# Four places for the attention chunks, their halves loaded from two queues, and the sign of the float64 weights carried by a leaky ScalarE function

## The chip, the cores and the metric

The kernel runs on one core of one Trainium2 chip. A core has five engines, each with its own instruction stream in order: PE (TensorE, matrix products), DVE (VectorE), ACT (ScalarE), POOL (GpSimd) and SP (SyncE, which here only starts transfers). Sixteen DMA engines move data between the chip's memory and the core's on-chip memory. The engines wait for each other through counting semaphores. The metric is the device time of one execution in microseconds; lower is better.

## What is computed

Three parts run one after the other. A retention layer (attention with a decay in place of the softmax), a dense layer pair with a sigmoid GELU, and a soft mixture of experts:

```python
scores = scale * np.matmul(q, k.transpose(0, 1, 3, 2))      # q, k, v: (8, 8, 576, 64) float32
ret = scores * Dmat                                          # gamma_h ** (i - j) for j <= i, else 0
x = np.matmul(ret, v)                                        # -> x: (4608, 512)
h = x @ w_in                                                 # (512, 2048)
g = h * (1.0 / (1.0 + np.exp(-1.702 * h)))
y = g @ w_out                                                # (2048, 512)
logits = y @ phi                                             # (512, 32)
slot_input = softmax(logits, over tokens).T @ y              # (32, 512), 4 slots for each of 8 experts
slot_out[e] = np.maximum(slot_input[e] @ w1[e], 0.0) @ w2[e] # w1 (8, 512, 1024), w2 (8, 1024, 512)
out = softmax(logits, over slots) @ slot_out                 # (4608, 512)
```

`w_in` and `w_out` come as float64: their generator multiplies a float32 array by a float64 scalar. The kernel turns them into float32 itself, from the two 32-bit halves of each number.

## The kernel before

The 4608 tokens are worked on in 12 blocks of 384. A block needs six attention chunks of 64 tokens (72 chunks in all, 9 for each of the 8 batch entries) and sixteen feature steps (fc 0 to 15, 128 hidden features each).

**A chunk.** `load_chunk(g)` brings the chunk's queries, keys and values into one of the places `packs`: the lower 64 partitions with one DMA (line 171), the upper 64 with another (line 172). `scores(g)` makes the products Sp on PE (lines 183, 184), the scaled keys kt on POOL (187) and the decayed scores on DVE (189, 190), written over the queries. `chunk_out(g)` makes Op on PE (197, 198), scales it into xs on DVE (204), rounds it on ACT (205) and makes the remainder on POOL (206). `state(g)` adds to the running state St on PE (223, 224), and DVE writes the scaled state into the next chunk's place (226, 227). `chunk(g)` runs `chunk_out(g)` and `state(g)`, starts the load of chunk g+3 into the place that chunk g has left, and then runs `scores(g+1)`.

**A feature step.** `main_fc` runs twelve products hp on PE (line 328) and the GELU on ACT into gT (330). Three hp tiles are in use in turn. `turn_fc` turns gT with three DVE transposes (351). After eight steps sixteen small DMAs on SP's queue (357, the "nat block" below) put the turned pieces into `nat`, which the slot product Sg (412) reads in the next block.

**The weights.** `load_raw` loads 512 KB of float64 numbers into one of eight places (six in `early_raw`, two in `raw`). `load_w_in` (16 times) scales the upper words on ACT (276), and DVE shifts the lower words (277), joins the two (278), and puts the sign bit back (279). ACT then rounds the result (282), and POOL or DVE makes the remainder (283; the letters `I` and `Id` in the order below choose). `make_wp` (8 times, two `w_out` pieces each) makes a sign with ACT (293), scales with ACT (294), shifts and joins on DVE (295, 296) and multiplies by the sign on POOL or DVE (297, `O` or `Od`). PE transposes the piece (302, tpw), ACT copies it (303), ACT starts a DMA that keeps the piece in memory (305), and PE and DVE make Wp = w_out phi (310, 312), which the logits Lg (364) need.

**The order.** The list `START` gives the order of the program for the first block: T a load of a chunk, C the constants cs, I a piece of w_in, O a pair of pieces of w_out, A a chunk, M a feature step of block 0. A scheduler then orders the instructions of all engines from that. Block 0 needs chunks 0 to 5 before its first product hp. In later blocks the chunks of block n+1 run between the feature steps of block n, after the steps in `CHUNK_AT`. All DMAs count on eight semaphores (DMAHW0 to DMAHW7) given out in turn over both queues. Before a DMA starts, its engine waits until the DMA that had the same semaphore last has landed.

## Time and profile before

| | us |
|---|---|
| median of three executions | 803.67 (803.54 to 805.54) |
| the profiled execution, its own time | 797.39 |
| its span, first to last instruction | 795.6 |
| PE busy in the span | 727.0 (91%) |
| DVE, ACT, POOL busy | 391.0, 245.4, 186.2 |

The profiled execution is 6.3 us shorter than the median of the others. The span has three parts: a start, in which the weights and the first chunks are prepared and block 0 is worked on (the first product hp begins at 55.2 us), eleven blocks that look alike (to some 664 us), and an end with the experts. PE is the busiest engine by far, and it works nearly without a gap from 60 us on.

### The profile page before, as it was taken

The numbers are of one execution on the slowest core, as the hardware profiler recorded it, in microseconds if no ns is written. First come the engines' busy times: TensorE is split into PE (matmuls) and PEld (weight loads), VectorE is DVE, ScalarE is ACT, GpSimd is POOL, SyncE is SP. The second block draws the span as 40 slices with busy tenths as digits, with TensorE's granted clock in tenths as the row PEclk, the third lists the DMA queues.
The fourth block names the chain that finished last, engine by engine and source line by source line (L and its number), as shares of the span: only waits on it lengthen the run. The fifth ranks groups of instructions, "written<-read, shape, count | busy, mean of one in ns | idle before, by whom it ended". The sixth has DMA issues, their size and how long they took to land.

```text
span 795.6 us, 18020 instructions
## 1 busy us (share of the span) xinstructions
PE 727.0 (91%) x7288; PEld 589.8 (74%) x7288; DVE 391.0 (49%) x1152; ACT 245.4 (31%) x479; POOL 186.2 (23%) x255
## 2 busy tenths in 40 slices
PE   3359999999999999999999999998998999997994
PEld 3247788788788878887888788878877798772453
DVE  3999964545445535454454454543543542222223
ACT  2446552323123223231132232411311323431323
POOL 5664661121221121212221212121122110001000
PEclk9999899999999999999999999999999999998997
DMA  9998867575355644744555447435544559898978
GB/s 230 283 297 247 266 168 187 128 157 130 80 122 122 135 106 106 159 114 96 119 125 132 111 105 160 116 85 119 134 97 99 124 126 324 278 379 341 408 307 325
DMA packets 78003, 142.19 MB, mean 179 GB/s; under 512 B 10720, under 2 KB 52960, under 8 KB 77920
## 3 DMA queue, kind: packets, MB, share of 16 engines
q1 hardware_dynamic: 75616, 136.85, 62.8%
q10 hardware_dynamic: 2304, 4.20, 1.5%
q8 instruction: 57, 0.93, 0.5%
q14 instruction: 26, 0.21, 0.1%
HBM read 92.77 MB, written 13.63 MB: 134 GB/s over the span
## 4 chain that ended last, share of the span: by engine, by line
PE 63%; SPq 15%; DMA 9%; DVE 9%; issue 3%; ACT 1%; POOL 0%; DVEq 0%; POOLq 0%; ACTq 0%
PE hp L328 38%; SPq L357 13%; DMA pack<-in_qkv_dram 8%; PE Sg L412 4%; PE Lg L364 4%; PE Op L197 2%; PE Sp L184 2%; PE h_ps L589 2%; PE so_ps L653 2%; PE St L223 1%; DMA early_raw<-in_moe_w_in_dram 1%; PE op L671 1%; DVE early_raw L278 1%; SPq L171 1%; PE St L224 1%
## 5 line engine op out<-in xcount | busy, mean ns | idle before, releaser
L328 PE MATMUL hp<-x,w 128*128 128x384 f32 x2304 | 445.3, 346 | 2.2 <-ACT x L205 2.2
L328 PEld LDWEIGHTS hp<-x,w 128*128 128x128 f32 x2304 | 399.8, 191 | 32.8 <-issue 10.6
L330 ACT ACTIVATE gT<-hp 128x384 f32<-128x384 f32 x192 | 93.9, 490 | 299.0 <-PE hp L328 297.9
L187 POOL TENSOR_TENSOR kt<-pack,cs 64x256 f32<-64x256 f32 x128 | 83.1, 649 | 215.2 <-DMA pack<-in_qkv_dram 138.8
L351 DVE STREAM_TRANSPOSE ring<-gT 128x128 f32<-128x128 f32 x240 | 55.9, 284 | 127.1 <-ACT gT L330 127.1
L351 DVE STREAM_TRANSPOSE pre<-gT 128x128 f32<-128x128 f32 x288 | 65.4, 281 | 81.3 <-ACT gT L330 77.9
L206 POOL TENSOR_TENSOR x<-xs,x 128x256 fp32r<-128x256 f32 x72 | 56.4, 783 | 195.9 <-ACT x L205 195.1
L197 PEld LDWEIGHTS Op<-pack 128*64 128x64 f32 x576 | 42.2, 144 | 37.4 <-issue 23.8
L205 ACT CAST x<-xs 128x256 fp32r<-128x256 f32 x72 | 29.1, 405 | 126.3 <-DVE xs L204 126.1
L183 PE MATMUL Sp<-pack 128*64 128x64 f32 x576 | 51.9, 233 | 16.9 <-DMA pack<-in_qkv_dram 11.4
L197 PE MATMUL Op<-pack 128*64 128x64 f32 x576 | 53.3, 236 | 12.0 <-DVE pack L189 12.0
L183 PEld LDWEIGHTS Sp<-pack 128*64 128x64 f32 x576 | 43.2, 146 | 18.9 <-issue 11.5
L223 PE MATMUL St<-pack,kt 128*64 128x64 f32 x512 | 47.2, 234 | 9.4 <-DVE pack L227 7.8
L184 PE MATMUL Sp<-pack 128*64 128x64 f32 x576 | 50.3, 233 | 5.6 <-DMA pack<-in_qkv_dram 5.6
L198 PE MATMUL Op<-pack 128*64 128x64 f32 x576 | 51.4, 236 | 0.0
L223 PEld LDWEIGHTS St<-pack,kt 128*64 128x64 f32 x512 | 38.7, 146 | 14.5 <-POOL kt L187 8.9
L364 PE MATMUL Lg<-gT,Wp 128*32 128x384 f32 x384 | 46.5, 502 | 2.5 <-DVE Wp L312 2.5
L184 PEld LDWEIGHTS Sp<-pack 128*64 128x64 f32 x576 | 42.3, 146 | 8.0 <-DMA pack<-in_qkv_dram 7.7
L224 PE MATMUL St<-pack,kt 128*64 128x64 f32 x512 | 44.8, 234 | 0.0
L198 PEld LDWEIGHTS Op<-pack 128*64 128x64 f32 x576 | 41.6, 145 | 0.7 <-DVE pack L190 0.5
L189 DVE TENSOR_TENSOR pack<-Sp,cs 64x256 f32<-64x256 f32 x72 | 30.6, 424 | 19.7 <-PE Sp L184 13.9
L224 PEld LDWEIGHTS St<-pack,kt 128*64 128x64 f32 x512 | 37.6, 147 | 2.6 <-issue 2.6
(125 smaller groups left out, 644.4 us busy)
## 6 DMA issues: line engine op xcount, KB each, us to landing
pack<-in_qkv_dram SPq DMA_DIRECT2D x144, 256.0 KB, 4.7
wx<-in_moe_w_dram SPq DMA_DIRECT2D x56, 512.0 KB, 8.6
nat<-pre SPq DMA_DIRECT2D x192, 96.0 KB, 2.2
nat<-ring SPq DMA_DIRECT2D x160, 96.0 KB, 2.2
out_dram<-ob SPq DMA_DIRECT2D x18, 512.0 KB, 3.4
early_raw<-in_moe_w_in_dram SPq DMA_DIRECT2D x13, 512.0 KB, 9.9
early_raw<-in_moe_w_out_dram SPq DMA_DIRECT2D x11, 512.0 KB, 7.4
wo_dram<-ring ACTq DMA_DIRECT2D x16, 256.0 KB, 6.2
```

The lines of the kernel that those rows point to most:

```text
L183: pe.matmul(Sp[C:128, p, :], t[:, KTA, p], t[:, Q0, p], start=True, stop=True)
L184: pe.matmul(Sp[0:C, p, :], t[:, KTB, p], t[:, Q1, p], start=True, stop=True)
L187: pool.tensor_tensor(kts[g % 2][r0:r0 + C, h], t[r0:r0 + C, KN], ksc[r0:r0 + C, cb, :].unsqueeze(2).to_broadcast([C, NP, D]), op=ALU.mult)
L197: pe.matmul(Op[0:C, p, :], t[:, V0, p], t[:, Q0, p], start=True, stop=True)
L198: pe.matmul(Op[C:128, p, :], t[:, V1, p], t[:, Q1, p], start=True, stop=True)
L223: pe.matmul(s_[0:C, p, :], kk[:, 0, p], t[:, V0, p], start=first, stop=True, skip_group_check=True)
L224: pe.matmul(s_[C:128, p, :], kk[:, 1, p], t[:, V1, p], start=first, stop=True, skip_group_check=True)
L328: pe.matmul(hp, wt[fc][:, a, dc, :], b[n][:, dc, :], start=(i == 0), stop=(i == 3 * NDC - 1))
L330: act.activation(gT[n, g][:, fl, :], hp, AF.Gelu_apprx_sigmoid)
L351: dve.transpose(dst[:, c], src[:, c])
L357: sp.dma_start(nat[n][32 * b:32 * b + 32, :, a, hf * HF:(hf + 1) * HF, :], pre[n, hf][32 * a:32 * a + 32, b])
L364: pe.matmul(Lg[n][32 * fl:32 * fl + 32, :], Wp[:, g * GF + fl, :], gT[n, g][:, fl, :], start=(g == 0), stop=(g == NFC // GF - 1))
```

## The change

- There are four places for chunks (`NPACK` 4), and the load of chunk g+3 stands at the beginning of `chunk(g)`, into the place of chunk g-1.
- The upper half of each chunk is loaded by ACT's queue, the lower half by SP's as before.
- The first two places are set to zero by DVE, the other two by POOL.
- The float64 weights are scaled by ACT's Prelu in place of Copy. It multiplies negative numbers by a further 2^32, which puts a bit into the exponent that the join's shift by three moves to the sign bit. So the DVE step that put the sign back (279), the ACT sign (293) and the product with it (297) are gone, and for `w_out` the scaling is written over the raw piece instead of into the ring.
- There are seven raw places instead of eight, and at the end of the program one place more in `pw2` and one less in `raw`. `Od` in START is now `O`.

```diff
-NW2 = 8
+NW2 = 9
-NPACK = 3
+NPACK = 4
...
-        pool.memset(t[0:C, 0:KN], 0.0)
-        pool.memset(t[C:128, KTA:7], 0.0)
+        own = dve if i < 2 else pool
+        own.memset(t[0:C, 0:KN], 0.0)
+        own.memset(t[C:128, KTA:7], 0.0)
...
         sp.dma_start(t[0:C, KN * PC:7 * PC], qkv[g, 0:C])
-        sp.dma_start(t[C:128, 0:KTA * PC], qkv[g, C:128])
+        act.dma_start(t[C:128, 0:KTA * PC], qkv[g, C:128])
...
     def chunk(g):
 
+        if g + NPACK - 1 < NT // C:
+            load_chunk(g + NPACK - 1)
         chunk_out(g)
         state(g)
-        if g + NPACK < NT // C:
-            load_chunk(g + NPACK)
         if g + 1 < NT // C:
             scores(g + 1)
...
-        if i % 8 < 6:
-            raw = early_raw[:, i % 8]
+        if i % 7 < 6:
+            raw = early_raw[:, i % 7]
         else:
-            raw = px.tile([128, 1024], F32, tag="raw", name="raw", bufs=2)
+            raw = px.tile([128, 1024], F32, tag="raw", name="raw", bufs=1)
...
-            act.activation(w, w, AF.Copy, scale=2.0 ** -112)
+            act.activation(w, w, AF.Prelu, scale=2.0 ** -112, alpha=2.0 ** 32)
             dve.tensor_scalar(lower, lower, 29, None, op0=ALU.logical_shift_right)
-            dve.scalar_tensor_tensor(lower, upper, 3, lower, op0=ALU.logical_shift_left, op1=ALU.bitwise_or)
-            dve.scalar_tensor_tensor(upper, upper, -2147483648, lower, op0=ALU.bitwise_and, op1=ALU.bitwise_or)
+            dve.scalar_tensor_tensor(upper, upper, 3, lower, op0=ALU.logical_shift_left, op1=ALU.bitwise_or)
...
-                bits, sign = wo.bitcast(I32), free
-                act.activation(sign, upper.bitcast(F32), AF.Sign)
-                act.activation(wo, upper.bitcast(F32), AF.Copy, scale=2.0 ** -112)
+                act.activation(upper.bitcast(F32), upper.bitcast(F32), AF.Prelu, scale=2.0 ** -112, alpha=2.0 ** 32)
                 dve.tensor_scalar(lower, lower, 29, None, op0=ALU.logical_shift_right)
-                dve.scalar_tensor_tensor(bits, bits, 3, lower, op0=ALU.logical_shift_left, op1=ALU.bitwise_or)
-                (pool if how["mul"][i] else dve).tensor_tensor(wo, wo, sign, op=ALU.mult)
+                dve.scalar_tensor_tensor(wo.bitcast(I32), upper, 3, lower, op0=ALU.logical_shift_left,
+                                         op1=ALU.bitwise_or)
...
-                    for i in range(2):
-                        prefetch(place_in(px, "raw", 2))
+                    prefetch(place_in(px, "raw", 1))
```

The scheduler's order moves with it. On DVE, in the start, these rows stand around the decayed scores of chunk 3. In the kernel before chunk 3 is in `pack_93` (its scores are lines 189 and 190), and what stands ahead of them, behind the output of chunk 2 (line 204), is this:

```order
L204 TENSOR_TENSOR xs<-Op,cs 128x256
L278 SCALAR_TENSOR_TENSOR early_raw<-early_raw 128x512
L295 TENSOR_SCALAR raw<-raw 128x512
L296 SCALAR_TENSOR_TENSOR ring<-ring,early_raw 128x512
L277 TENSOR_SCALAR raw<-raw 128x512
L279 SCALAR_TENSOR_TENSOR early_raw<-early_raw 128x512
L296 SCALAR_TENSOR_TENSOR ring<-ring,raw 128x512
L278 SCALAR_TENSOR_TENSOR raw<-raw 128x512
L189 TENSOR_TENSOR pack_93<-Sp,cs 64x256
L190 TENSOR_TENSOR pack_93<-Sp,cs 64x256
```

In the changed kernel, whose line numbers differ by one or two, chunk 3 is in `pack_102`, and the same stretch reads:

```order
L205 TENSOR_TENSOR xs<-Op,cs 128x256
L280 SCALAR_TENSOR_TENSOR early_raw<-early_raw 128x512
L190 TENSOR_TENSOR pack_102<-Sp,cs 64x256
L191 TENSOR_TENSOR pack_102<-Sp,cs 64x256
L294 TENSOR_SCALAR early_raw<-early_raw 128x512
```

Seven weight steps stood between the two chunks' rows, and one does now. From the first decayed scores to the xs of chunk 5 there are 68 DVE instructions before and 57 now (lines of the kernel before: 189 and 190 six and seven times, 226 and 227 six and six, 204 six and six, 277 nine and seven, 278 eight and seven, 279 seven and none, 283 four and four, 295 six and four, 296 four and three). On PE the first hp stands behind Op of chunks 0 to 5 in both; the St of chunk 5 and the Sp of chunk 6 now stand ahead of it.

On SP, in the blocks that look alike, around the nat block of block 2's first half (`x16`). Before, with the load of chunk 24 in `pack_93` behind it:

```order
L171 DMA pack_99<-in_qkv_dram 64x1024
L172 DMA pack_99<-in_qkv_dram 64x1024
L357 DMA nat<-pre 32x3x256 x16
L171 DMA pack_93<-in_qkv_dram 64x1024
L172 DMA pack_93<-in_qkv_dram 64x1024
L171 DMA pack_96<-in_qkv_dram 64x1024
```

And now, where chunk 24 is in `pack_93` too:

```order
L172 DMA pack_99<-in_qkv_dram 64x1024
L172 DMA pack_102<-in_qkv_dram 64x1024
L172 DMA pack_93<-in_qkv_dram 64x1024
L356 DMA nat<-pre 32x3x256 x16
L172 DMA pack_96<-in_qkv_dram 64x1024
```

The load of chunk 24 has moved ahead of the sixteen DMAs, and chunk 25 (`pack_96`) is now the first behind them. It is the same at all such places from the fourth nat block on.

On ACT the loads of the upper halves now stand between the GELUs. Here is the stretch with the load of chunk 26 (`pack_99`), with the semaphores that each row waits for:

```order
L329 ACTIVATE gT<-hp 128x384 [waits PE_49] x2
L206 CAST x<-xs 128x4x64 [waits DVE_49]
L173 DMA pack_99<-in_qkv_dram 64x1024 [waits DMAHW5_49,DMAHW6_49,PE_49,Pool_49]
L329 ACTIVATE gT<-hp 128x384 [waits PE_49]
L329 ACTIVATE gT<-hp 128x384 [waits PE_49,Activation_49]
```

The count of DMAHW6 that this load waits for is that of the sixth DMA of the nat block shown above, which SP starts. It stands behind the GELU of step 10 of that block, and the nat block can begin after the GELU of step 7. The loads of the upper halves of other chunks wait in the same way for the sixth, twelfth or last DMA of a nat block, and the first, sixth and eleventh DMA of a nat block wait for an upper half to land.

## Rows read from the trace of the kernel before

**Rows 1.** The page: its first line, and the engines' busy time with their share of the span and number of instructions.
```profile
span 795.6 us, 18020 instructions
...
PE 727.0 (91%) x7288; PEld 589.8 (74%) x7288; DVE 391.0 (49%) x1152; ACT 245.4 (31%) x479; POOL 186.2 (23%) x255
```

**Rows 2.** Five stretches of the span: from and to, length, busy time and instructions of PE, PEld, DVE, ACT and POOL, the granted share of TensorE's clock, the DMA engines' share and GB/s.
```profile
0.00:8.60 8.60, 1.57 (x16) 1.22 (x16) 0.68 (x1) 1.28 (x1) 5.81 (x14) 1.00 0.73 166
8.60:55.20 46.60, 19.93 (x275) 17.20 (x275) 41.80 (x69) 17.52 (x30) 26.47 (x25) 1.00 1.06 285
55.20:128.00 72.80, 69.87 (x823) 59.04 (x824) 61.30 (x136) 42.12 (x78) 42.78 (x41) 0.95 0.80 238
128.00:664.00 536.00, 524.16 (x5288) 440.75 (x5287) 252.16 (x863) 141.62 (x280) 108.27 (x172) 0.99 0.53 122
...
80.00:90.00 10.00, 9.09 (x76) 6.96 (x78) 9.91 (x19) 4.42 (x9) 6.51 (x7) 0.66 0.77 267
```

**Rows 3.** PE's waits from 0 to 128 us: for whom, us in total, how often, the longest.
```profile
PE Op L197 <- DVE pack L189: 12.0, 5, 4.1
PE St L223 <- DVE pack L227: 7.8, 4, 4.4
...
PE Lg L364 <- DVE Wp L312: 2.5, 1, 2.5
```

**Rows 4.** PE's waits from 128 to 664 us, all that there are.
```profile
PE Sp L183 <- DMA pack<-in_qkv_dram: 7.4, 9, 1.5
PE Sp L184 <- DMA pack<-in_qkv_dram: 4.4, 6, 0.8
```

**Rows 5.** DVE's groups of instructions between 8.6 and 55.2 us: count, then busy us and mean ns of one, then idle time before them.
```profile
L279 DVE SCALAR_TENSOR_TENSOR early_raw<-early_raw 128x512 int32<-128x512 int32 x7 | 6.2, 892 | 0.0
L277 DVE TENSOR_SCALAR early_raw<-early_raw 128x512 int32<-128x512 int32 x8 | 4.9, 617 | 2.3 <-DMA early_raw<-in_moe_w_in_dram 2.3
L278 DVE SCALAR_TENSOR_TENSOR early_raw<-early_raw 128x512 int32<-128x512 int32 x7 | 4.8, 688 | 0.4 <-ACT early_raw L276 0.3
L295 DVE TENSOR_SCALAR early_raw<-early_raw 128x512 int32<-128x512 int32 x4 | 4.6, 1155 | 0.1
L283 DVE TENSOR_TENSOR w<-early_raw,w 128x512 fp32r<-128x512 f32 x4 | 3.1, 782 | 0.0
L227 DVE TENSOR_TENSOR pack<-St,cs 64x256 f32<-64x256 f32 x6 | 2.6, 427 | 0.1
L189 DVE TENSOR_TENSOR pack<-Sp,cs 64x256 f32<-64x256 f32 x6 | 2.6, 426 | 4.9 <-DMA cs<-in_consts_dram 4.8
L204 DVE TENSOR_TENSOR xs<-Op,cs 128x256 f32<-128x256 f32 x6 | 2.5, 422 | 1.6 <-PE Op L198 1.5
L190 DVE TENSOR_TENSOR pack<-Sp,cs 64x256 f32<-64x256 f32 x6 | 2.5, 417 | 0.2
L296 DVE SCALAR_TENSOR_TENSOR ring<-ring,early_raw 128x512 int32<-128x512 int32 x3 | 2.5, 818 | 0.0
L226 DVE TENSOR_TENSOR pack<-St,cs 64x256 f32<-64x256 f32 x6 | 2.4, 407 | 0.0
```

**Rows 6.** PE in order of time around 28 us: start us, length us, what; in brackets the idle time before it.
```profile
28.63 0.45 PE L183 MATMUL Sp<-pack 128*64 128x64 f32 x2 [4.00 <-DMA pack<-in_qkv_dram]
```

**Rows 7.** DVE in order of time around 35 us, in the same columns.
```profile
33.40 1.75 DVE L279 SCALAR_TENSOR_TENSOR early_raw<-early_raw 128x512 int32<-128x512 int32 x1
...
36.80 0.43 DVE L189 TENSOR_TENSOR pack<-Sp,cs 64x256 f32<-64x256 f32 x1
```

**Rows 8.** PE in order of time, around the first products hp and at 80 us.
```profile
55.19 0.69 PE L328 MATMUL hp<-x,w 128*128 128x384 f32 x1 [2.15 <-ACT x L205]
...
58.56 2.79 PE L328 MATMUL hp<-x,w 128*128 128x384 f32 x11
...
80.91 1.49 PE L364 MATMUL Lg<-gT,Wp 128*32 128x384 f32 x4 [2.46 <-DVE Wp L312]
82.33 4.21 PE L328 MATMUL hp<-x,w 128*128 128x384 f32 x12
```

**Rows 9.** The chain that ended last, in order of time: start us, length us, what.
```profile
227.21 4.36 PE hp L328 x24
...
547.46 5.93 PE hp L328 x24
...
602.87 5.85 PE hp L328 x24
```

**Rows 10.** SP's queue in order of time around one nat block: start us, length us of the issue, what.
```profile
210.31 11.22 SPq L357 DMA_DIRECT2D nat<-pre  x16
221.64 0.54 SPq L171 DMA_DIRECT2D pack<-in_qkv_dram  x1
222.28 0.55 SPq L172 DMA_DIRECT2D pack<-in_qkv_dram  x1
```

**Rows 11.** PE in order of time behind that nat block.
```profile
225.47 0.30 PE L183 MATMUL Sp<-pack 128*64 128x64 f32 x2 [0.67 <-DMA pack<-in_qkv_dram]
```

**Rows 12.** The page's DMA issues: count, KB each, median us from issue to landing.
```profile
pack<-in_qkv_dram SPq DMA_DIRECT2D x144, 256.0 KB, 4.7
...
nat<-pre SPq DMA_DIRECT2D x192, 96.0 KB, 2.2
```

**Rows 13.** ACT in order of time during that nat block.
```profile
217.05 0.49 ACT L330 ACTIVATE gT<-hp 128x384 f32<-128x384 f32 x1 [1.59 <-PE hp L328]
```

More of the change, by code (lines that the diff above doesn't have):

```diff
@@ L38 @@
 HF = NFC // 2
-NW2 = 8
+NW2 = 9
 NW3, NW4 = 6, 5
 DH = DM // 2
-NPACK = 3
+NPACK = 4
 PC = NP * C
 START = (
-    "T0 C T1 Id T2 P A A Id A I A A I A Id A M O I M A Id M O I M I A M Od I M I A M O Id M I A M O I M Id A M O I "
+    "T0 C T1 Id T2 P A A Id A I A A I A Id A M O I M A Id M O I M I A M O I M I A M O Id M I A M O I M Id A M O I "
     "M A M O M M O M"
@@ L171, in load_chunk @@
         sp.dma_start(t[0:C, KN * PC:7 * PC], qkv[g, 0:C])
-        sp.dma_start(t[C:128, 0:KTA * PC], qkv[g, C:128])
-    how = {"sub": {}, "mul": {}}
+        act.dma_start(t[C:128, 0:KTA * PC], qkv[g, C:128])
+    how = {"sub": {}}
     St = {}
@@ L471, in step @@
         elif x[0] == "O":
-            how["mul"][8 - len(outs)] = x != "Od"
             outs.pop(0)()
```

## The prediction

> **What bounds the kernel now.** I began with the page's first lines: PE is busy for 727.0 of 795.6 us [rows 1], so the change can only win where PE stands still or runs slowly. The table by stretches says where that is [rows 2]. Between 8.6 and 55.2 us PE has 19.9 us of work in 46.6, from 55.2 to 128 it has 69.9 in 72.8, and from 128 to 664 it has 524.2 in 536. In the end, behind 664 us, the change only swaps one place for another, so I leave that part alone.
>
> Next I asked what PE waits for in each stretch. In the start it is DVE: 12.0 us for the decayed scores, 7.8 us for the scaled state [rows 3]. DVE is busy for 41.8 of those 46.6 us [rows 2]: it is the bound. One example shows how. The scores of chunk 3 are made from 28.63 us [rows 6], but DVE gets to them at 36.80, behind weight steps such as a 1.75 us sign step [rows 7]. The DMA engines are also full there, with a share of 1.06 [rows 2], which I return to. From 128 us on, all of PE's waits are for chunks that have not landed, 7.4 + 4.4 = 11.8 us [rows 4], which accounts for the whole of the 11.8 us that PE lacks. SP's rows show the reason: the nat block holds SP's queue from 210.31 for 11.22 us, chunk 24's halves start at 221.64 and 222.28 [rows 10], and PE wants them before they land [rows 11].
>
> **The start, up to the first hp.** The first hp begins at 55.19 us, on the output of chunk 5 [rows 8]. DVE's way to that output is 68 instructions before and 57 now. I price both lists by the means of this stretch [rows 5]. Before: 9 x 0.617 + 8 x 0.688 + 7 x 0.892 + 6 x 1.155 + 4 x 0.818 + 4 x 0.782 + 6 x 2.099 (one each of 189, 190, 204, 226, 227) = 43.2 us. Now: 7 x 0.617 + 7 x 0.688 + 4 x 0.782 + 4 x 1.155 + 3 x 0.818 + 7 x 0.843 + 6 x 1.256 = 32.8 us. The difference is 10.4 us, of which the sign steps are 6.2 and the rest is weight work that now stands behind chunk 5. The lower bound is about 3 us, if DVE then waits for transfers (first rival). The upper bound is 17 us: if the two shift lines, which are the same operation, both took the time of the cheaper one, 4 x 0.538 = 2.2 us more would go, and the 4.8 us in which DVE is now idle might go too. I take 10.4, because DVE, which gives this number, is the engine that is full.
>
> The constants are issued one SP issue earlier, but four upper halves compete with them on the second queue from the first moment. Four halves are 1.0 MB, at 285 GB/s 3.7 us [rows 2, 12]. DVE waits 4.8 us for these constants [rows 5], so a later landing is paid in full: between -0.6 and 3.7, I take 1 us of loss.
>
> DVE's four new memsets cover 64x768. The nearest row writes 64x256 in 0.426 us [rows 5], so each takes at most 1.3 us and all four at most 5.1. DVE has 0.68 us of work up to 8.6 us [rows 2], and that idle time hides them. Prelu I price like the Copy it replaces, one ACT instruction of the same shape; ACT is busy for 17.5 of 46.6 us [rows 2], so a dearer one would be hidden as well.
>
> **The start, from the first hp on.** Here PE is nearly full, so what it has to do moves forward as a whole. One Sp and one St group of a chunk are already done by then; I count 1 us for them. One stall remains that DVE's load causes: 2.46 us for Wp, after which twelve hp take 4.21 us [rows 8] where they take half of 4.36 elsewhere [rows 9]. In those 10 us the granted clock is 0.66 [rows 2]. So 2.5 + 2.0 = 4.5 us hang on Wp coming late. DVE has 11 sign steps and products fewer in this stretch, but its order is new there as well, so I take half, 2 us. The bounds are 4.5 and a new stall of the same size, -4.5.
>
> **The eleven blocks.** Chunk 24 is now started ahead of the nat block, and so are the other chunks that PE waited for. The first chunk behind the block is now one that PE needs a chunk later, that is up to four feature steps of some 2.2 us (half of 4.36) [rows 9], against the 0.7 us that were missing [rows 11]. The upper halves no longer queue on SP at all. I take the whole 11.8 us; the bounds are 6, if only the upper halves come in time, and 11.8. At 547 us twenty-four hp take 5.93 us in place of 4.36 [rows 9], behind such a wait. At 602.87 us it is 5.85 [rows 9]. Together that is 3 us. Few of the fifteen waits [rows 4] were followed by this, so I take half, 1.5, with bounds 0 and 3.
>
> ACT now starts 72 transfers, each shorter than 0.6 us to issue like SP's [rows 10]. It is busy for 31% of the span [rows 1], so the cover is its own idle time in front of each GELU, 1.59 us in the row shown [rows 13]. If the cover were gone, PE would pay up to 72 x 0.6 = 43 us. The wait that comes with them is the third rival. What stands behind a waiting load on ACT is the next GELU, for which PE's three hp tiles wait.
>
> **The sum.** 10.4 - 1 + 1 + 2 + 11.8 + 1.5 = 25.7 us. Against the profiled execution's own 797.4 us this gives 771.7; against the median of 803.67, which lies 6.3 above it, 778.0. I give the second.
>
> **A rule on the second queue.** At the start the DMA engines' share is 1.06 at 285 GB/s [rows 2]. The Trainium skill, DMA: Bandwidth & Descriptors, section Issuing engines are not separate DMA queues, says that transfers from any engine run on the same 16 DMA engines, and that a second issuing engine saves only the time to issue. By that rule the second queue brings the start nothing. The trace of before cannot decide it, since only SP loads chunks there; my sum gives the second queue nothing in the start either, but the first rival is what the rule would mean if the engines were the bound.
>
> **A rule on DVE and POOL.** The shift of line 295 takes 1.155 us in the mean and that of line 277 takes 0.617, for the same shape [rows 5], while POOL is busy for 26.5 us of the stretch [rows 2]. The Trainium skill, SBUF — State Buffer, section SBUF: two separate sides, says that DVE and POOL lock each other out of a shared pair of ports for a whole instruction. By that rule the sign products that leave POOL shorten DVE's other steps as well, and the sum would be up to 2 us larger.
>
> **The rivals.**
> 1. The transfers bound the start. For: the share of 1.06. Against: up to the first hp the new order needs seven chunks, seven pieces of w_in and two of w_out, 3.7 + 3.7 + 1.0 MB and 0.5 of constants, 8.9 MB; at 285 GB/s that is 31 us, against 45 in my forecast. If they decide nevertheless, 3 us remain of the 10.4 and nothing of the 2: 803.7 - (3 + 11.8 + 1.5) + 1 - 1 = 787.4 us.
> 2. Everything goes well: the first hp comes 17 us earlier, the stall on Wp goes whole, and both slow stretches go. 17 + 1 + 4.5 + 11.8 + 3 - 1 = 36.3, so 767.4 us. Against it: every term stands at its end.
> 3. Slower: ACT is caught behind the nat block. The load of chunk 26 waits on ACT for the block's sixth copy. By before's rows that copy is issued near 210.3 + 5 x 0.70 = 213.8 and lands 2.2 us later [rows 10, 12], at 216.0, and ACT would reach it at 217.5 [rows 13]: 1.5 us to spare. PE is covered by two further hp tiles, 2 x 2.2 us. So PE loses only from the point where the copies come 1.5 + 4.4 = 5.9 us later against the GELUs. At 7.5 us each of some 19 nat blocks would cost 1.6 us, 30 us in all: 778 + 30 = 808 us.
> 4. The chunks are late in another way: the waits of rows 4 stay, since the lower halves still queue on SP. Then the start alone is gained: 803.7 - 12.4 = 791.3 us. Against it is the order: the chunk that was late now stands ahead of the block.
>
> **How the numbers follow.** My forecast has a chance of 0.65 with its own range of 772 to 785; rival 1 has 0.14, rival 2 has 0.10, rival 3 has 0.05, rival 4 has 0.06. The range from 766 to 792 takes in the forecast, rivals 1, 2 and 4, and leaves out rival 3 and the ends of the others. A change of under 0.3%, 2.4 us, is about what a measurement of this kernel cannot tell from none. Rival 3 alone is slower; from its 0.05 I give 0.01 to the middle, and 0.01 more for gains that cancel from the other cases: faster 0.94, the same 0.02, slower 0.04.
>
> **What would show it.** The first hp near 45 us and the 193rd (block 1's first) some 13 us earlier than before; no PE wait for a chunk behind 128 us; ACT's waits on loads below a us; lines 279 and 297 gone and DVE below nine tenths by 90 us. The prediction is wrong if the first hp stays beyond 50 us with PE waiting for DMA, if PE waits for ACT's GELU in the blocks, or if DVE's order in the start makes a new stall of several us.

## The result, and the profile of the changed kernel

The changed kernel takes 769.9 us (median of four runs, 768.96 to 770.63) against 803.6 for the kernel before beside it: a ratio of 0.9575, with a 95% interval of 0.9556 to 0.9594. The forecast was 778.0 in a range of 766 to 792. The profiled execution takes 770.2 us of its own; before's took 797.4, so 27.2 us went between the two profiles, where the sum had 25.7. The other 6.6 us of the miss come from the medians: before's three runs lay 6.3 us above its profiled execution, the changed kernel's lie 0.3 below. In four later sets of 7 to 13 runs the kernel before had medians of 798.4 to 802.1, with single runs from 790.4 to 806.8. So the profiled execution of before was an ordinary run, and the 6.3 us that the forecast added lie within the scatter of that kernel.

The page's lines that answer to [rows 1]:

```profile
span 768.4 us, 18070 instructions
...
PE 714.9 (93%) x7288; PEld 581.8 (76%) x7288; DVE 379.2 (49%) x1138; ACT 234.8 (31%) x463; POOL 159.9 (21%) x239
```

The table by stretches, cut where block 1 and the tail now begin, with ten more microseconds around the first products hp and the columns of [rows 2]:

```profile
8.60:55.20 46.60, 22.34 (x318) 20.20 (x319) 32.23 (x65) 15.72 (x28) 21.06 (x27) 0.66 1.06 277
50.00:60.00 10.00, 8.50 (x66) 8.08 (x66) 7.12 (x12) 5.08 (x9) 5.02 (x5) 0.64 1.06 290
55.20:120.00 64.80, 62.81 (x783) 53.17 (x783) 46.02 (x102) 34.18 (x65) 25.20 (x26) 0.98 0.92 272
120.00:635.00 515.00, 515.00 (x5279) 434.95 (x5278) 262.19 (x881) 140.25 (x279) 106.48 (x171) 1.00 0.56 125
```

In the blocks PE stands still no more: 515.00 busy in 515.00, and the view of waits has no row at all for 120 to 640 us, where [rows 4] had 11.8 us. DVE in the start fell from 41.8 to 32.2 us [rows 2]. One thing stands in the first row that the prediction has no term for: the granted clock is 0.66 where before has 1.00 [rows 2]. It falls between 20 and 30 us, where PE is busy for 3.6 of the ten, is 0.50 from 30 to 50 us (the lower of its two levels, 1.2 in place of 2.4 GHz), and is back at 1.00 from 60 us on. No run here separates what that costs. PE's waits up to 120 us, to be laid beside [rows 3]:

```profile
PE hp L327 <- ACT x L206: 10.4, 1, 10.4
PE Op L198 <- DVE pack L190: 9.3, 5, 3.2
PE Sp L184 <- DMA pack<-in_qkv_dram: 7.6, 2, 7.1
PE St L224 <- DVE pack L228: 3.9, 2, 3.1
PE Lg L363 <- DVE Wp L311: 1.1, 2, 0.9
```

The first row is new: one wait of 10.4 us, for the cast of x in front of the first hp. Read from PE in order of time, the two kernels part like this (us):

| | before | changed | difference |
|---|---|---|---|
| first hp | 55.2 | 51.5 | -3.7 |
| first hp to the 193rd (block 1) | 72.75 | 68.6 | -4.2 |
| last GELU of block 0 to that of block 10 | 534.6 | 515.2 | -19.3 |
| the rest | 133.1 | 133.1 | 0.0 |

The stretch from block 1 to 664 us of the kernel before, counted ahead as eleven blocks, holds ten, block 1 to block 10; block 11 lies in the rest. The prediction's term for the eleven blocks is therefore measured on these ten.

**Where the new wait comes from.** ACT in order of time in the changed kernel, from 34 us on:

```profile
34.50 0.68 ACT L278 ACTIVATE early_raw<-early_raw 128x512 f32<-128x512 f32 x1
39.68 0.33 ACTq L304 DMA_DIRECT2D wo_dram<-ring  x1
44.31 0.47 ACTq L173 DMA_DIRECT2D pack<-in_qkv_dram  x1
44.83 0.41 ACT L206 CAST x<-xs 128x256 fp32r<-128x256 f32 x1 [9.65 <-DMA early_raw<-in_moe_w_in_dram]
45.14 0.64 ACT L283 CAST w<-early_raw 128x512 fp32r<-128x512 f32 x1
45.69 0.65 ACT L278 ACTIVATE early_raw<-early_raw 128x512 f32<-128x512 f32 x1
```

DVE in the same time:

```profile
38.98 0.43 DVE L228 TENSOR_TENSOR pack<-St,cs 64x256 f32<-64x256 f32 x1
46.37 1.54 DVE L280 SCALAR_TENSOR_TENSOR early_raw<-early_raw 128x512 int32<-128x512 int32 x1 [6.96 <-ACT early_raw L278]
...
50.60 0.41 DVE L205 TENSOR_TENSOR xs<-Op,cs 128x256 f32<-128x256 f32 x1
```

ACT computes nothing between 35.2 and 44.8 us. At 39.68 it issues a store; next in its queue is the upper half of chunk 8, which starts at 44.31. Each was held (the word used below for an issue that its engine cannot start yet, so that everything behind it in the engine's order waits too). The store waited for a semaphore whose last transfer was a piece of w_out that SP issued at 28.63 and that landed at 39.60. The load carries a wait for a DMA completion semaphore, and the last transfer that used the same semaphore is a piece of w_in that SP issued at 33.43. SP's row of it (it merges two issues), and then the DMA issues of the stretch from 33.4 to 33.7 us, whose last number is the time to landing:

```profile
33.43 1.62 SPq L266 DMA_DIRECT2D early_raw<-in_moe_w_in_dram  x2
```

```profile
early_raw<-in_moe_w_in_dram SPq DMA_DIRECT2D x1, 512.0 KB, 10.8
```

33.43 + 10.8 = 44.23, and 0.08 later ACT goes on. Everything queued behind the load waited with it: a cast of x, a cast of w, the Prelu of the next piece, which had landed at 36.29. DVE was done at 39.4 and then waited 6.96 us for that Prelu. The load held ACT from 40.0 to 44.3, so by an estimate from these rows 4.3 of the 6.96 us are its doing, and 2.7 that of the store in front of it; the output of chunk 5 (line 205) came at 50.60 and the first hp at 51.50.

### The profile page after: what moved, and what is told of

Read it like the earlier page. It is cut to its first block, busy times and chain, and to the rows that moved or that the text cites. A ratio compares the mean times of both kernels' runs of the same rounds, so it can differ in the third digit from the quotient of the medians.

```text
span 768.4 us, 18070 instructions
## 1 busy us (share of the span) xinstructions
PE 714.9 (93%) x7288; PEld 581.8 (76%) x7288; DVE 379.2 (49%) x1138; ACT 234.8 (31%) x463; POOL 159.9 (21%) x239
## 3 DMA queue, kind: packets, MB, share of 16 engines
q10 hardware_dynamic: 8064, 23.07, 12.1%
## 4 chain that ended last, share of the span: by engine, by line
PE 85%; DVE 2%; ACT 1%; issue 1%; DVEq 0%; ACTq 0%
PE hp L327 53%; PE Lg L363 5%; PE Sg L411 5%; PE Op L198 4%; PE Sp L185 3%; PE St L224 3%; PE h_ps L586 2%; PE so_ps L650 2%; PE op L668 1%; PE St L225 1%; PE lt L373 1%; PE tpg L339 1%; PE Op L199 1%; PE Sp L184 1%; PE cp L622 1%; PE dp L398 1%
## 5 line engine op out<-in xcount | busy, mean ns | idle before, releaser
L327 PE MATMUL hp<-x,w 128*128 128x384 f32 x2304 | 438.8, 344 | 11.2 <-ACT x L206 10.4
L327 PEld LDWEIGHTS hp<-x,w 128*128 128x128 f32 x2304 | 396.5, 189 | 40.0 <-ACT gT L329 13.1
L207 POOL TENSOR_TENSOR x<-xs,x 128x256 fp32r<-128x256 f32 x72 | 54.1, 752 | 154.0 <-ACT x L206 153.7
L184 PE MATMUL Sp<-pack 128*64 128x64 f32 x576 | 48.0, 229 | 7.6 <-DMA pack<-in_qkv_dram 7.6
L185 PE MATMUL Sp<-pack 128*64 128x64 f32 x576 | 48.5, 230 | 0.0
L184 PEld LDWEIGHTS Sp<-pack 128*64 128x64 f32 x576 | 41.5, 144 | 7.7 <-issue 7.1
L225 PE MATMUL St<-pack,kt 128*64 128x64 f32 x512 | 44.8, 233 | 0.0
L185 PEld LDWEIGHTS Sp<-pack 128*64 128x64 f32 x576 | 41.5, 143 | 0.3 <-issue 0.3
L411 PE MATMUL Sg<-nat,dn 128*32 128x512 f32 x288 | 37.4, 626 | 0.3 <-DVE dn L400 0.3
```

The source lines that it names most:

```text
L184: pe.matmul(Sp[C:128, p, :], t[:, KTA, p], t[:, Q0, p], start=True, stop=True)
L185: pe.matmul(Sp[0:C, p, :], t[:, KTB, p], t[:, Q1, p], start=True, stop=True)
L225: pe.matmul(s_[C:128, p, :], kk[:, 1, p], t[:, V1, p], start=first, stop=True, skip_group_check=True)
L327: pe.matmul(hp, wt[fc][:, a, dc, :], b[n][:, dc, :], start=(i == 0), stop=(i == 3 * NDC - 1))
L411: pe.matmul(Sg[32 * b:32 * b + 32], dn[n][:, c, :], nv[:, 4 * b:4 * b + 4], start=(c == 0), stop=(c == NT128 - 1))
```

## The experiments

Three parts are told apart: new or old sign steps, three or four places, one or two queues. "Four places" takes in what goes with them: the earlier load, the new zeroing and the seven raw places. The experiments are short edits of the changed kernel or of the one before. Of the eight combinations seven were run; old sign steps with three places and two queues were not. What they gave, with "hp" for the first hp, "block 1" for the 193rd, and "ten" for ten blocks as in the table above:

| kernel | sign | places | queues | median us | hp | block 1 | ten |
|---|---|---|---|---|---|---|---|
| before | old | 3 | 1 | 803.6 | 55.2 | 127.9 | 534.6 |
| e3 | new | 3 | 1 | 793.0 | 52.1 | 121.5 | 537.2 |
| e10 | new | 3 | 2 | 777.1 | 54.4 | 120.9 | 518.9 |
| e11 | old | 4 | 1 | 776.0 | 50.2 | 128.3 | 513.0 |
| e4 | old | 4 | 2 | 782.6 | 55.2 | 134.7 | 516.8 |
| e2, e8 | new | 4 | 1 | 764.3, 762.2 | 45.0, 42.5 | 117.6, 115.5 | 513.4 |
| changed, e7 | new | 4 | 2 | 769.9, 769.8 | 51.5 | 120.1 | 515.2 |

**e1, the start's upper halves on SP.**

```
-        act.dma_start(t[C:128, 0:KTA * PC], qkv[g, C:128])
+        (act if g < 4 or g >= 15 else sp).dma_start(t[C:128, 0:KTA * PC], qkv[g, C:128])
```

> The changed kernel with one difference: the upper halves of chunks 4 to 14 (those loaded in the start) go back to SP's queue; ACT keeps the first four and those of the blocks. Theory A, the held queue: in the changed kernel ACT stood still from 39.68 to 44.31 us in front of chunk 8's upper half, whose completion semaphore was last used by a piece of w_in that SP issued at 33.43 and that takes 10.6 us to land; casts, GELU inputs and the output of chunk 5 stood behind it. Without it the first hp comes 4.6 to 7 us earlier, at 44 to 47 us, and the kernel takes 763 to 766 us. Rival, full DMA engines: their share is 0.99 between 25 and 50 us, so chunks and weights come no sooner whoever issues them; the first hp stays at 50 to 53 us and the kernel at 769 to 772 us. The ten blocks stay at 515 us by both.

Measured: 769.2 us (768.87 to 774.19), the first hp at 50.36. By the numbers the rival won, but ACT's rows show that the hold had only moved, to a store of a piece of w_out:

```profile
41.82 1.42 ACT L293 ACTIVATE early_raw<-early_raw 128x512 f32<-128x512 f32 x2
48.93 0.33 ACTq L304 DMA_DIRECT2D wo_dram<-ring  x1
49.36 0.65 ACT L278 ACTIVATE early_raw<-early_raw 128x512 f32<-128x512 f32 x1 [6.12 <-DMA pack<-in_qkv_dram]
```

The store's semaphore was last used by a lower half that SP issued at 37.07 and that took 11.8 us to land: 48.87. The output of chunk 5 was ready on DVE at 46.43, and ACT cast it at 49.92, behind the store:

```profile
46.02 0.41 DVE L205 TENSOR_TENSOR xs<-Op,cs 128x256 f32<-128x256 f32 x1
```

```profile
49.92 0.39 ACT L206 CAST x<-xs 128x256 fp32r<-128x256 f32 x1
```

So a hold delayed the first hp here too, but since it stayed, the total of e1 could not decide between hold and full engines.

**e2, one queue.**

```
-        act.dma_start(t[C:128, 0:KTA * PC], qkv[g, C:128])
+        sp.dma_start(t[C:128, 0:KTA * PC], qkv[g, C:128])
```

> The changed kernel with both halves of every chunk on SP; the four places and the chunk's load ahead of the nat block stay. Theory A, the order: the eleven blocks were won by starting a chunk ahead of the nat block, not by the second queue. PE still waits for no chunk behind 120 us, the ten blocks take 515 to 517 us, and with ACT free in the start the kernel takes 763 to 767 us. Rival, the second queue: the upper halves queue on SP again and are late again; half of the loss comes back, 6 to 10 us, the ten blocks take 521 to 525 us and the kernel 770 to 778 us.

Measured: 764.3 us (760.86 to 768.05); the first hp at 44.98, ten blocks in 513.4, no wait for a chunk behind 120 us. Theory A holds: no chunk was late, the total lies in its range, and the ten blocks came even shorter than its 515 to 517. With the fourth place the second queue is not needed in the blocks, and in the start it costs.

**e3, the sign alone**, from the kernel before (and the same for w_out, lines 292 to 297):

```
-            act.activation(w, w, AF.Copy, scale=2.0 ** -112)
+            act.activation(w, w, AF.Prelu, scale=2.0 ** -112, alpha=2.0 ** 32)
...
-            dve.scalar_tensor_tensor(lower, upper, 3, lower, ...)
-            dve.scalar_tensor_tensor(upper, upper, -2147483648, lower, ...)
+            dve.scalar_tensor_tensor(upper, upper, 3, lower, ...)
```

> The kernel before with one difference: the leaky function in place of the sign steps (lines 278, 279 and 292 to 297); three places, both halves on SP, eight places for raw weights. Theory A: DVE's list up to the first hp was the bound of the start, so the first hp comes 6.2 us (the sign steps of w_in alone) to 10.4 us earlier, at 45 to 49 us; the waits for chunks in the blocks stay at 11.8 us shown; the kernel takes 803.6 - 12 = 791 us, between 788 and 796. Rival, full DMA engines: DVE gets free but waits for pieces of w_in and chunks; the first hp at 52 us or later, the kernel at 798 to 803 us.

Measured: 793.0 us (789.77 to 802.29 in ten runs), ratio 0.9932 (0.9888 to 0.9977); the first hp at 52.13. The total lies in A's range, the first hp does not: it came 3.1 us earlier in place of 6 to 10. PE's longest waits up to 128 us:

```profile
PE Sp L183 <- DMA pack<-in_qkv_dram: 10.6, 3, 8.8
PE St L223 <- POOL kt L187: 5.8, 1, 5.8
PE Sp L183 <- POOL pack L160: 5.5, 1, 5.5
```

With 0.8 us at line 184 that is 11.4 us for chunks, where before has 5.1. The wait of 8.8 us is for chunk 3, at which before lost 4.0 [rows 6]; but the chunk was no later than before (28.25 us against 28.63), PE only came to it sooner. ACT was held, by stores of line 302:

```profile
36.82 0.65 ACT L281 CAST w<-raw 128x512 fp32r<-128x512 f32 x1 [9.29 <-DMA early_raw<-in_moe_w_out_dram]
48.25 0.40 ACT L205 CAST x<-xs 128x256 fp32r<-128x256 f32 x1 [6.54 <-DMA raw<-in_moe_w_out_dram]
```

DVE's own waits, from its first decayed scores to the output of chunk 5, say where the missing us went:

```profile
DVE early_raw L278 <- ACT early_raw L276: 8.6, 3, 6.1
```

Before, that wait was 0.3 us [rows 5]. DVE was busy for 30.8 us in this stretch in place of 41.3, 10.5 less, and idle for 13.1 in place of 4.8. So waiting for the held ACT took back 8.3 us of the 10.5; for a late chunk DVE did not wait at all.

**e4, the old sign steps**: the diff of e3 the other way round, in the changed kernel, with `Od` back in START.

> The changed kernel with the sign steps of the kernel before; four places, two queues and the early load stay. Theory A: the blocks' gain stays whole (19.4 us for ten blocks), the start gains 0 to 3 us, since DVE is full there again: 781 to 785 us, first hp at 53 to 56 us. Rival, the start's gain came from the second queue and the fourth place and not from DVE: first hp near 51.5 us and the kernel at 770 to 775 us.

Measured: 782.6 us (781.89 to 784.11), the first hp at 55.24, ten blocks in 516.8. Theory A, with 17.8 of the blocks' 19.4 us. Beside the changed kernel's 769.9 the new sign steps are worth 12.7 us with four places.

**e5, no transfer on ACT**, from e2:

```
-                act.dma_start(wo_dram[fc // 2, :, fc % 2, :], wo)
+                pool.dma_start(wo_dram[fc // 2, :, fc % 2, :], wo)
```

> The kernel of e2 (all loads on SP) with one more difference: the stores of w_out's pieces (line 304) are issued by POOL and no longer by ACT, so that ACT issues no transfer at all in the start. Theory A, as e1 and e2 left it: it is any transfer on ACT's queue that holds ACT, a store as well as an upper half, since it waits until the earlier transfer with the same completion semaphore has landed. In e1 ACT stood from 43.24 to 48.93 us in front of a store, in e2 three times before a store, 3.63 + 2.35 + 2.69 = 8.7 us, with DVE waiting for ACT behind it only some 1.6 us of these up to the first hp. So ACT's waits in front of line 304 go, the wait of 3.8 us for the ring copy (line 302) behind the first hp goes, the first hp comes at 42 to 45 us, block 1 some 3 to 6 us earlier than in e2, and the kernel takes 758 to 762 us. Rival, full DMA engines (share 1.07 up to 55 us): ACT waits for pieces of w_in in place of semaphores, block 1 comes within 1 us of e2's 117.6, and the kernel takes 763 to 766 us.

Measured: 764.1 us (763.58 to 766.58), the first hp at 42.82, block 1 at 114.98. The first hp came as theory A said, block 1 hardly (2.6 us before e2, 0.5 before e8), and the total is e2's, 1.9 us above e8's beside it. The holds of stores that were left in e2, the longest from 48.2 to 54.5 us, do not set the time.

**e6, the upper halves on POOL**: the line of e2 with `pool` in place of `sp`.

> The changed kernel with the upper halves issued by POOL in place of ACT; two queues stay. Theory A, the held engine: the second queue costs nothing by itself, what it costs is ACT standing still; with POOL as its engine the hold falls on POOL, behind which only products of kt and remainders of x stand: first hp at 44 to 48 us and 762 to 767 us. Rival, the competition: upper halves that start early on a second queue take the DMA engines from pieces of w_in and from the constants, whoever issues them: first hp at 50 to 53 us, 768 to 772 us. If POOL is slow at issuing (its issue is not in any trace so far) both could be later.

Measured: 767.3 us (764.9 to 770.68), the first hp at 49.48, which fits neither. It answers another question than it asked: POOL starts the first load behind its memsets, and PE gets the upper half of chunk 0 late.

```profile
5.17 2.22 POOL L173 DMA_DIRECT2D pack<-in_qkv_dram  x4
```

PE's view has an 8.31 us wait for it, until 14.30. Inconclusive on the hold.

**e7 and e8, the changed kernel and e2 side by side.**

> The changed kernel itself once more, beside the others of this call on the same chip: 769 to 771 us by every theory, first hp at 51.5 us with ACT standing in front of chunk 8's upper half for 4 to 5 us.

> The kernel of e2 once more beside the changed kernel: theory A says that one queue for the chunks is 4 to 7 us faster than two in the same call (763 to 766 against 769 to 771 us); the rival, that e2's 764.3 was the chip it ran on, says that both are within 2 us here.

Measured: 769.8 us (768.01 to 771.05) and 762.2 (760.31 to 763.83), in one set with e5. The ranges are 4 us apart. One queue with four places is 7.7 us faster than the changed kernel; its ratio to before is 0.9523 (0.9477 to 0.9569), the changed kernel's here 0.9625 (0.9584 to 0.9665).

**e9, the first four upper halves on ACT, no hold.** e5 with `act if g < 4 else sp`.

> The kernel of e5 (ACT issues no transfer later on, the stores go out on POOL) with the upper halves of the first four chunks on ACT, as in the changed kernel; each of these four is the first transfer with its completion semaphore and so waits for none. It has the competition of four early upper halves without the hold. Theory A, the hold: first hp at 42 to 45 us as in e5 (42.8), the kernel at 762 to 766 us. Rival, the competition: the four halves that start at 0.7 us push back the constants and the first pieces of w_in, and all behind them: first hp at 48 to 51 us, near e1's 50.4, the kernel at 766 to 770 us.

Measured: 767.8 us (766.25 to 768.57), the first hp at 46.13, block 1 at 120.96. Both matter. Without a transfer that holds ACT the first hp comes 5.4 us before the changed kernel's; against e5 the four early halves cost 3.3 us there and 6.0 at block 1. DVE's first decayed scores show how it begins, first here, then in e5:

```profile
10.76 0.43 DVE L190 TENSOR_TENSOR pack<-Sp,cs 64x256 f32<-64x256 f32 x1 [5.46 <-DMA cs<-in_consts_dram]
```

```profile
8.04 0.43 DVE L190 TENSOR_TENSOR pack<-Sp,cs 64x256 f32<-64x256 f32 x1 [3.39 <-DMA cs<-in_consts_dram]
```

The constants land 2.7 us later when four halves start beside them. Later on, four waits for GELU cost PE 6.3 us here (1.8 in e5): ACT stands in front of a Prelu whose piece has not landed, and a GELU is queued behind it.

**e10, the second queue without the fourth place**: e3 with `act` for `sp` at the upper half (line 172).

> The kernel of e3 (three places, the leaky function) with the upper halves on ACT: the second queue without the fourth place. Theory A, the place and the order: a load can start only when the chunk's place is free, behind the nat block as before; PE's waits for chunks from 128 us on stay between 6 and 13 us (12.9 in e3) and ten blocks take 525 us or more; ACT is held in the start as in the changed kernel; 785 to 795 us. Rival, the queue: upper halves no longer stand behind the nat block on SP, the waits fall below 4 us, ten blocks take 515 to 520 us and the kernel 770 to 778 us.

Measured: 777.1 us (776.08 to 781.10), ten blocks in 518.9. The rival won. PE's waits from 128 us on, first in e10, then in e3, which has one queue:

```profile
PE Sp L183 <- DMA pack<-in_qkv_dram: 1.4, 3, 0.6
```

```profile
PE Sp L184 <- DMA pack<-in_qkv_dram: 6.5, 6, 2.1
PE Sp L183 <- DMA pack<-in_qkv_dram: 6.4, 9, 1.1
```

The lower halves came no earlier behind the nat block. That of chunk 24 was issued right behind the block and landed 4.1 us later (3.7 in e3), and PE still waited for it:

```profile
216.64 1.13 PE L325 MATMUL hp<-x,w 128*128 128x384 f32 x5
...
218.04 0.24 PE L183 MATMUL Sp<-pack 128*64 128x64 f32 x1 [0.27 <-DMA pack<-in_qkv_dram]
```

But the second wait, for the upper half, is gone, and the new order puts five products hp in front of the chunk's Sp that stood behind it before. So there are two remedies for the late chunks, and either takes nearly all of the waits: a place more, or the upper halves on another queue. The change has both, and pays for the second one in the start. Ten blocks are still 5.5 us longer here than with a fourth place and one queue.

**e11, the old sign steps with four places and one queue.**

> The kernel of e2 and e8 (four places, early load, all loads on SP) with the sign steps of the kernel before: what four places are worth alone. Theory A: DVE bounds the start with the old sign steps whoever issues the loads, so that the sign is worth as much here as beside e4 (782.6 against 769.8, 12.8 us): 773 to 777 us, first hp at 53 to 56 us, no wait for a chunk behind 128 us. Rival: the sign is worth only what e3 showed alone (some 5 us of 798): 766 to 769 us, first hp below 50 us.

Measured: 776.0 us (775.68 to 776.58), ten blocks in 513.0, block 1 at 128.3. Total and blocks are theory A's; the first hp at 50.17 fits neither well. The new sign steps are worth 12 to 14 us here, some of it behind the first hp. Four places alone take some 25 us off (801.5 for before beside it).

**e12, small stores**, from e2:

```
-                act.dma_start(wo_dram[fc // 2, :, fc % 2, :], wo)
+                act.dma_start(wo_dram[fc // 2, :, fc % 2, 0:32], wo[:, 0:32])
...
-            src = wo_dram[key[1]] if wide else ...
+            src = w1[0, 0:128, :].rearrange("p (c d) -> p c d", c=2) if wide else ...
```

> The kernel of e2 and e8 (four places, all loads on SP) with fewer bytes in the start: each of the 16 stores of w_out's pieces writes 32 of its 512 columns, 16 in place of 256 KB, and the pieces read back in the end come from w1 in place of the stored ones (that part of the computation is left out; the number of transfers, their issues and the order of the instructions' kinds stay). Some 13 of the stores are issued before 95 us, 13 x 240 KB = 3.1 MB, at e8's 300 GB/s some 10 us of the engines' time. Theory B, which e1 to e11 suggest, that without the sign steps the transfers bound the start from the first chunk to block 1 (share 1.04 to 1.07 up to 100 us in e8, and block 1 between 115 and 123 us wherever the first hp lies between 42 and 54): block 1 comes 5 to 10 us earlier than e8's 115.5, at 105 to 111 us, and the kernel takes 752 to 758 us. Rival, the engines' order (DVE, ACT and the semaphores) bounds it: block 1 within 2 us of 115.5 and the kernel at 760 to 764 us.

Measured: 766.6 us (766.12 to 769.53), block 1 at 118.3. Theory B falls as it was put: block 1 came 0.7 us later than in e2 and 2.8 later than in e8, not 5 to 10 earlier. But the engines' share hardly moved. Three stretches of e12, then of e8:

```profile
40.00:60.00 20.00, 14.05 (x114) 12.53 (x115) 11.22 (x23) 8.49 (x14) 6.20 (x8) 0.66 1.05 248
60.00:80.00 20.00, 19.05 (x236) 15.76 (x234) 19.38 (x42) 12.27 (x24) 10.35 (x9) 1.00 1.03 270
80.00:100.00 20.00, 17.17 (x230) 14.44 (x232) 18.39 (x42) 12.70 (x26) 8.44 (x9) 1.00 0.97 252
```

```profile
40.00:60.00 20.00, 13.07 (x117) 11.53 (x118) 11.07 (x22) 7.79 (x13) 5.69 (x7) 0.83 1.07 274
60.00:80.00 20.00, 19.48 (x253) 15.84 (x251) 18.83 (x50) 12.04 (x23) 9.56 (x9) 1.00 1.05 307
80.00:100.00 20.00, 19.39 (x241) 16.64 (x239) 16.01 (x34) 12.96 (x26) 8.95 (x10) 1.00 1.04 312
```

The bytes fell by a tenth to a fifth (last number), the engines' share (the one before it) by 0.02 to 0.07. The stores themselves did take less. Their queue over the whole run, its packets, MB and share of the 16 engines' span, first in e12, then in e8:

```profile
q10 hardware_dynamic: 2304, 0.26, 0.3%
```

```profile
q10 hardware_dynamic: 2304, 4.20, 1.6%
```

1.3% of the span is some 10 us of the engines, the dose that was meant. The other transfers took part of it up: the same 75616 packets of the main queue went from 65.6% to 66.4%. A share near 1 goes with 270 GB/s in e12 as well as with 307 in e8, so it does not say that the engines could move no more. The order of instructions also moved with the shorter stores. What sets block 1 between 115 and 123 us, once DVE is relieved, stays open.

## Why the prediction was right, step by step

The sum was 25.7 us, and the two profiles are 27.2 apart. That it came within 1.5 us is luck: up to the first hp 3.7 us were gained where the prediction has 9.4, from there to block 1 4.2 where it has 3, in the blocks 19.3 where it has 13.3. The median lies in the range of 766 to 792, but outside the 772 to 785 of the forecast alone.

**The eleven blocks, 11.8 + 1.5 = 13.3 us; measured 19.3.** The mechanism was right and the size too small: what mis-sized it was taking a wait's length for its price. Before, from the last St product of the late chunk to the next hp:

```profile
224.57 0.22 PE L224 MATMUL St<-pack,kt 128*64 128x64 f32 x1
...
226.53 0.27 PE L184 MATMUL Sp<-pack 128*64 128x64 f32 x1 [0.77 <-DMA pack<-in_qkv_dram]
...
227.14 1.14 PE L328 MATMUL hp<-x,w 128*128 128x384 f32 x5
```

The same two places with nothing to wait for, in the changed kernel:

```profile
216.61 0.22 PE L225 MATMUL St<-pack,kt 128*64 128x64 f32 x1
...
217.23 0.44 PE L327 MATMUL hp<-x,w 128*128 128x384 f32 x1
```

2.57 us against 0.62: the chunk's two waits cost 1.95 us, while the brackets show 0.67 [rows 11] + 0.77 = 1.44. Some 0.26 us more at each wait pass while the profile counts PE as busy. If all fifteen waits are like these two, that makes 3.8 us; both slow stretches [rows 9], with a granted clock of 0.72 and 0.73 over six microseconds, went whole (1.00 in the blocks now), 3.0 us instead of 1.5. By this estimate 11.8 + 3.8 + 3.0 = 18.6 of the 19.3. The reason that was given, "the chunk starts ahead of the nat block", holds (e2, e8, e11). Its lower bound, 6 us "if only the upper halves come in time", was wrong: e10 has just that and takes 18.3 us off e3's 537.2, since the lower half's wait shrinks as well once five products hp stand in front of it.

**The first hp, 10.4 - 1 us; measured 3.7.** This is the term that failed. DVE's list was rightly taken for the bound, and priced a little low: from the first decayed scores to the output of chunk 5 DVE is busy for 28.1 us where before has 41.3, 13.2 less and not 10.4. But its idle time there rose from 4.8 to 12.1 us, 7.0 of them in front of one Prelu. With no loads on ACT the first hp is at 42.5 to 45.0 (e2, e5, e8), 10 to 13 us earlier, against "near 45". Five of these come with four places alone (e11), and the new sign steps add 5 to 8 where 6.2 were priced. What failed is the price of nothing for ACT's 72 loads. Only the time to issue them was weighed, and rival 3 (ACT caught at a load through another transfer) was looked for behind the nat block alone. It struck in the start, 4.3 us in front of chunk 8, right behind a store that was held for 4.4, and DVE stood 7.0 us behind the two. In the blocks it did not strike: ACT's waits there have no row on a DMA.

**The constants, 1 us; measured 2.2**, inside the bounds: DVE's first scores come at 10.86 where before has 8.64. e9 shows the early upper halves as the cause.

**From the first hp to block 1, 1 + 2 us; measured 4.2.** The wait for Wp went from 2.5 [rows 3] to 1.1 us, and the stretch of 80 to 90 us has a granted clock of 1.00 where it had 0.66 [rows 2]. Against that, the first products hp now run slowly: 50 to 60 us has 0.64, where before has 1.00 up to 80 us. The step that "what PE has to do moves forward as a whole" is loose, though: e5's first hp is 8.7 us before the changed kernel's, and block 1 only 5.1.

**The marks.** No wait for a chunk behind 128 us: seen. The 193rd hp came 7.9 us earlier, not 13; ACT waited 4.3 us at a load, not below one; DVE is busy for 9.3 of the 10 us from 80 on and for 8.8 from 90 on, so it fell below nine tenths about when it should. Of the signs that it is wrong, the first hp did stay beyond 50 us and a new stall of several us did come, but from ACT's queue and not from DVE's order. PE did not wait for ACT's GELU in the blocks.

**The rivals.** 1, transfers bound the start: the first hp came near its case, but by the hold, since in e8 the first hp came 9 us earlier with the engines as full (a share of 1.00 up to it, against 1.02). Full engines have a part in it all the same: the hold lasts until a landing, and that took 10.8 us. The rival's sum counts two pieces of w_out where DVE's list has four; with four the same estimate gives 9.9 MB and some 35 us, still less than 45. 2: only the blocks went that well. 3: the mechanism was real, the place was another. 4: refuted, no chunk was late.

**The two rules.** The second queue gave the start nothing: the engines moved 268 GB/s up to block 1 against 275 with one queue (e8). The Trainium skill, DMA: Bandwidth & Descriptors, section Issuing engines are not separate DMA queues, says that a second issuing engine saves only the time to issue. The start agrees, and e8 adds that it can cost 7.7 us. In e10 it saved some 16 us against e3, because the nat block alone takes SP 11.2 us to issue [rows 10], and the upper halves stood behind it no more. That is issue time too, but not a small one.

w_out's shift took 0.94 us in the mean before and 0.52 now (line 294, 16 steps up to block 1); w_in's stayed at 0.6. POOL lost its fourteen sign products, 1.45 us each, and is busy for 25.2 us from 55 us to block 1 in place of 42.8 [rows 2]. The Trainium skill, SBUF — State Buffer, section SBUF: two separate sides, says that a POOL instruction and a DVE instruction in a two-port mode, or one with two SBUF inputs, lock each other out of the shared ports, and that the one that starts first has them for its whole time. The rows of before agree, though none tells the mode of a shift. One shift of w_out, and the POOL instruction, a remainder of w_in, that was running when it began:

```profile
30.06 1.52 DVE L295 TENSOR_SCALAR raw<-raw 128x512 int32<-128x512 int32 x1
```

```profile
29.87 1.43 POOL L283 TENSOR_TENSOR w<-early_raw,w 128x512 fp32r<-128x512 f32 x1 [0.31 <-ACT w L282]
```

POOL is done at 31.30 and the shift 0.28 us later. Up to block 1 before, 14 of the 32 shifts took 0.38 to 0.43 us; the other 18 took 0.60 to 1.54, and each ended 0.28 to 0.29 us after a POOL instruction that it had met. In the changed kernel ten of 32 did. But the sign products are not what made w_out's shift dear: five of its six longest met a remainder of w_in, which the change leaves on POOL, and one a sign product. The shift got cheaper mostly because the new order makes it meet POOL less often.

## What to carry to other kernels

Before a load moves to a second engine, look at what that engine does next and at what each load waits for: its buffer, and also the transfer that used its completion semaphore last, which may be a slow one of another queue. Where late loads can be mended by one more buffer or by another queue, try each alone: here the buffer with one queue was 7.7 us faster than both. And price a wait of PE by comparing the same two instructions with and without it, not by the idle time in brackets.

## What the runs showed that was not expected

- An issue is held until an unrelated transfer lands, to within 0.1 us: 39.60 and 39.68 at a store of the changed kernel, 44.23 and 44.31 at a load, 48.87 and 48.93 at a store in e1.
- Kernels with late chunks scatter: before from 790.4 to 806.8 us in 38 runs, e3 from 789.8 to 802.3 in ten, against 768.0 to 771.1 in eight for the changed kernel. Why was not tried. The profiled execution of e1 was its longest by 5 us, with a granted clock of 0.92.
- With a sixteenth of the bytes in each store the DMA engines' share was still 1.05 and 1.03 from 40 to 80 us (e12), and the stores took 6.2 us to land in the median, against 7.9 in e8: the share did not follow the bytes.
